# Loading the first half of the last V tile ahead of V tiles 29 and 30

## Chip, cores, metric

The kernel runs on one core of a Trainium2 chip. The metric is the device time of one execution in microseconds (us); lower is better. Before the change it was 1277.38 us (median of 3 runs, 1277.30 to 1277.45).

## The reference, cut

One token of a block that mixes a grouped-query attention over a long cache with a small gated MLP:

```python
# x: [1, 1, 448], bf16; 16 query heads, 8 KV heads, 65536 cached tokens, head size 256
def A(x, k_cache, v_cache, wq, wo):          # caches: [1, 8, 65536, 256] bf16, 268 MB each
    q = (x @ wq).reshape(...)                # 16 heads
    p = softmax(q @ k.T / 16)                # over 65536 tokens
    return (p @ v).reshape(1, 1, 4096) @ wo
def B(x, W_gate, W_up, W_down):              # 448 -> 1792 -> 448, ReLU gate
    ...
g = sigmoid((x * gate_w).sum())
out = g * A(...) + (1 - g) * B(...)
```

What matters here: 537 MB of K and V have to be read once, and hardly anything is computed per byte. Below, K31 or V29 is a tile of the K or V cache, numbered from 0 to 31 over all heads, and wo is the weight of the output projection.

## The kernel before

K and V come as 64 tiles of 8 MB (128 partitions x 64 KB): four K tiles and four V tiles for each of the eight KV heads. Three buffers of that size (`ring[0..2]`) take them in turn. All large loads are issued by the sync queue, in one order, each when the last reader of its buffer is done. The tail of that order is what the change touches (code abbreviated):

```python
TILE = 19.35                                  # us a tile is expected to take; only orders things
order = [("wq", 0, 8.7), ("k", 0, TILE), ("gu", 0, 7.7), ("wd", 0, 3.8)]
for n in range(1, NT):                        # NT = 32
    order.append(("k", n, TILE))
    if n >= NTH - 1:                          # NTH = 4; V lags K by three tiles
        order.append(("v", n - (NTH - 1), TILE))
NW = H - 3
order += [("wo", 0, 7.3), ("v", NT - 3, TILE), ("v", NT - 2, TILE)]
PIECES = [(0, 64), (64, 96), (96, 112), (112, 120), (120, 128)]   # V tile 31 comes in pieces
for i, (lo, hi) in enumerate(PIECES):
    order.append(("vp", i, TILE * (hi - lo) / U))
# ... cut: four more wo pieces, the last heads ...

# which buffer: a tile gets the next in turn, and waits for that buffer's last reader
LASTS = (0, 1, 2, 0, 1, 0)
if kind in ("k", "v") or (kind, i) in (("wo", 0), ("vp", 0)):
    sl = ...
    slot[kind, i], freed[kind, i] = sl, held.get(sl, [])
    held[sl] = [(kind, i)]
# so: K31 in 0, V28 in 1, wo in 2, V29 in 0 (after K31), V30 in 1 (after V28), V31's pieces in 0 (after V29)
wo_sb = ring[slot["wo", 0]][:, 0:J * 2 * D]   # wo fills 14336 of a row's 32768 elements: the rest is free

# ... cut ...
dep = dma("sp", t, "r%d" % sl, lambda e: e.dma_start(ring[sl][:], v_src(n)), free(("v", n)))
# ... cut: pieces of V31 ...
dep = dma("sp", t, "vp%d" % i, lambda e: e.dma_start(
    ring[sl][:, lo * 256:hi * 256], v_src(n)[:, lo * 256:hi * 256]), free(("vp", 0)))
# wo: five loads; rows of 1792 bytes, 128 partitions x 2 or 1 or, the first, 10 of them
l_["wo", i] = dma("sp", t, "wo%d" % i, lambda e: e.dma_start(wo_sb[:, lo:hi, :, :], ...), free(("wo", 0)))
```

TensorE multiplies a V tile as soon as it has landed and the head's probabilities are ready; the very last work is the projection of the last head with the last wo piece, a copy, and the store of 896 bytes.

## Time and profile before

| | value | where it stands |
|---|---|---|
| time | 1277.38 us | median of the runs |
| span in the profile | 1276.1 us | page |
| share of the span in which the 16 DMA engines move the sync queue's packets | 99.7% | page, part 3 |
| read from memory | 549.03 MB, 430 GB/s | page, part 3 |
| TensorE, VectorE busy | 33%, 50% | page, part 1 |

From the page of the kernel before: the span, TensorE's busy time, the 40 slices of the DMA engines' busy share (tenths) and of their rate, the main queue, and the chain that ended last.

```profile
span 1276.1 us, 10216 instructions
...
PE 427.3 (33%) x4568; PEld 167.5 (13%) x4568; DVE 633.2 (50%) x421; ACT 63.3 (5%) x124; POOL 4.6 (0%) x21
...
DMA  9999999999999999999999999999999999999998
GB/s 401 448 427 428 436 431 440 433 429 431 436 438 436 428 429 438 436 436 429 429 438 431 438 433 429 433 436 434 436 431 429 436 433 436 433 431 436 405 446 354
...
q1 hardware_dynamic: 12930, 549.03, 99.7%
...
HBM read 549.03 MB, written 0.00 MB: 430 GB/s over the span
## 4 chain that ended last, share of the span: by engine, by line
DMA 2%; PE 1%; SPq 0%; issue 0%; DVE 0%
DMA ring<-in_A_wo_dram 2%; PE O L409 1%; SPq L554 0%; PE A_ps L389 0%; SPq L563 0%; DVE P_sb L582 0%
```

Every slice of the DMA row is a 9, which is the highest digit, until the last.

The sync queue's timeline in the tail (start, how long the issue took, line; an issue waits for a free buffer ahead of its start). L550 are whole V tiles, L554 the pieces of V31, L563 wo:

```profile
...
start us, us, engine line op out<-in xcount [idle before <-releaser]
1172.85 0.33 SPq L550 DMA_DIRECT2D ring<-in_A_v_cache_dram  x1
1173.22 0.44 SPq L563 DMA_DIRECT2D ring<-in_A_wo_dram  x1
1208.27 13.83 SPq L550 DMA_DIRECT2D ring<-in_A_v_cache_dram  x2
1238.01 2.34 SPq L554 DMA_DIRECT2D ring<-in_A_v_cache_dram  x5
1240.39 21.26 SPq L563 DMA_DIRECT2D ring<-in_A_wo_dram  x4
```

At 1208.27 us V29 is issued, when K31's buffer comes free (the row merges two issues; the second, V30, starts at 1221.77). Of the end of the chain of waits (start, length, what):

```profile
...
1241.26 31.47 DMA ring<-in_A_wo_dram
...
1272.77 1.68 PE A_ps L389 x10
...
1274.48 0.38 DVE P_sb L582
```

The last wo piece lands at 1273.86 us (table below), and only 2.2 us follow it; what ends the kernel is when the last pieces land.

The page's shares are means over 16 engines. The trace says more: a transfer runs on all 16 DMA engines, and each adds one to the transfer's semaphore when its part has landed. The Trainium skill says so too ("DMA: Bandwidth & Descriptors", "Why a DMA increments its semaphore by 16 and not by 1": the engines "finish independently"). From these sixteen increments I take the first, the mean and the last for each transfer, in us. This table is worked out from the trace, it is no view of the profile:

```
before            first     mean      last     last minus first
V28             1203.18   1204.19   1206.13    2.94
wo, 10 heads    1209.19   1210.13   1211.92    2.73
V29             1229.56   1230.01   1231.28    1.72
V30             1249.02   1249.54   1250.72    1.70
V31, half       1258.71   1259.25   1260.42    1.71
last wo piece   1272.25   1272.77   1273.86    1.60
```

The sixteen engines are not level: one is 2.9 us behind the first. And the spread falls from 2.73 to 1.72 us at V29, because the engines that lead had run dry before V29's packets came.

### The profile page before, as it was taken

Reading aid. Unit: us, or ns where it says so; the run is one execution under the profiler, and the core shown is the slowest. Engines: PE = TensorE matmul, PEld = TensorE weight load, DVE = VectorE, ACT = ScalarE, POOL = GpSimd, SP = SyncE. Lnnn points to the kernel's source line nnn. Section 1 sums busy time; section 2 is a strip of 40 time slices with the busy share of each in tenths; the row PEclk is TensorE's granted clock in tenths of the full one; section 3 lists DMA queues with packets and bytes.
Section 4 is the critical chain, followed back from the end, with each engine's and each line's share of the span. In section 5 each row is a group of like instructions: output and inputs, shape, how many; then the busy total and the mean of one; then the engine's idle time right before and its main releaser. Section 6 shows DMA issues by size and latency. Waiting matters only on the chain. (4 is left out here: it accounts for less than half of the span.)

```text
span 1276.1 us, 10216 instructions
## 1 busy us (share of the span) xinstructions
PE 427.3 (33%) x4568; PEld 167.5 (13%) x4568; DVE 633.2 (50%) x421; ACT 63.3 (5%) x124; POOL 4.6 (0%) x21
## 2 busy tenths in 40 slices
PE   3633322334123532224331343321333324233254
PEld 1501110111001210002110111110111101011021
DVE  2597633465533655434555444555434655335600
ACT  0001000010000100001000010000100001000000
POOL 1000000000000000000000000000000000000000
PEclk9656666656666575667656666656666656666576
DMA  9999999999999999999999999999999999999998
GB/s 401 448 427 428 436 431 440 433 429 431 436 438 436 428 429 438 436 436 429 429 438 431 438 433 429 433 436 434 436 431 429 436 433 436 433 431 436 405 446 354
DMA packets 12948, 549.22 MB, mean 430 GB/s; under 512 B 1283, under 2 KB 3590, under 8 KB 3974
## 3 DMA queue, kind: packets, MB, share of 16 engines
q1 hardware_dynamic: 12930, 549.03, 99.7%
q8 instruction: 8, 0.13, 0.0%
q14 instruction: 6, 0.05, 0.0%
q10 hardware_dynamic: 4, 0.00, 0.0%
HBM read 549.03 MB, written 0.00 MB: 430 GB/s over the span
## 5 line engine op out<-in xcount | busy, mean ns | idle before, releaser
L367 DVE STREAM_TRANSPOSE ring<-ring 128x2048 uint32<-128x2048 uint32 x256 | 565.4, 2275 | 398.9 <-DMA ring<-in_A_k_cache_dram 398.9
L378 PE MATMUL ST<-ring,xc 128*16 128x512 bf16 x2048 | 222.8, 608 | 745.5 <-PEq L86 745.5
L378 PEld LDWEIGHTS ST<-ring,xc 128*16 128x16 bf16 x2048 | 68.0, 120 | 886.1 <-issue 884.8
L409 PE MATMUL O<-ring,ptp 128*4 128x512 bf16 x2048 | 152.3, 461 | 32.9 <-DMA ring<-in_A_v_cache_dram 18.8
L494 ACT ACTIVATE P_sb<-ST,nmb 128x512 bf16<-128x512 f32 x32 | 45.2, 1412 | 1103.5 <-DVE nmb L492 1103.5
L492 DVE TENSOR_REDUCE nmb<-ST 128x1 f32<-128x512 f32 x32 | 22.1, 689 | 116.8 <-PE ST L378 116.8
L409 PEld LDWEIGHTS O<-ring,ptp 128*4 128x4 bf16 x2048 | 56.9, 100 | 128.1 <-issue 71.8
L419 DVE CAST o_sb<-O 128x512 bf16<-128x512 f32 x8 | 5.5, 692 | 76.8 <-PE O L409 76.8
L513 DVE TENSOR_TENSOR P_sb<-P_sb,hs 128x1024 bf16<-128x1024 bf16 x16 | 18.9, 1222 | 9.4 <-ACT hs L507 9.4
L518 PE MATMUL PT<-identb,P_sb 128*128 128x128 bf16 x128 | 16.2, 307 | 16.8 <-PEq L86 15.8
L459 PE MATMUL M_ps<-xT,ring 128*128 128x1 bf16 x84 | 9.5, 205 | 17.5 <-DMA ring<-in_B_W_up_dram 17.5
L518 PEld LDWEIGHTS PT<-identb,P_sb 128*128 128x128 bf16 x128 | 12.4, 138 | 19.2 <-issue 19.2
L527 ACT COPY ptp<-PT 128x256 bf16<-128x256 bf16 x32 | 10.3, 375 | 23.9 <-PE PT L518 23.9
L341 PE MATMUL QN<-ring,P_sb 128*128 128x512 bf16 x32 | 8.9, 446 | 3.8 <-DMA ring<-in_A_wq_dram 3.8
L459 PEld LDWEIGHTS M_ps<-xT,ring 128*128 128x128 bf16 x84 | 7.2, 152 | 18.1 <-issue 17.7
L494 ACT ACTIVATION_READ_ACCUMULATOR P_sb<-ST,nmb 128x1 f32 x32 | 8.4, 263 | 0.0
L462 PE MATMUL M_ps<-xT,ring 128*64 128x1 bf16 x56 | 7.8, 276 | 0.0
L442 DVE STREAM_TRANSPOSE scr<-P_sb 128x256 uint32<-128x256 uint32 x1 | 0.4, 445 | 13.1 <-ACT P_sb L441 13.1
L503 PE MATMUL M_ps<-identf,hs 128*2 128x128 f32 x8 | 2.5, 308 | 11.1 <-PEq L86 11.1
L539 DVE RECIPROCAL hs<-M_ps 128x2 f32<-128x2 f32 x8 | 1.4, 171 | 8.3 <-PE M_ps L538 8.3
L462 PEld LDWEIGHTS M_ps<-xT,ring 128*64 128x64 bf16 x56 | 5.4, 191 | 0.4
L389 PE MATMUL A_ps<-ring,attnT 128*1 128x224 bf16 x64 | 4.7, 304 | 0.6 <-DMA ring<-in_A_wo_dram 0.6
(74 smaller groups left out, 66.2 us busy)
## 6 DMA issues: line engine op xcount, KB each, us to landing
ring<-in_A_v_cache_dram SPq DMA_DIRECT2D x1, 4096.0 KB, 22.4
ring<-in_A_wq_dram SPq DMA_DIRECT2D x1, 3072.0 KB, 10.4
ring<-in_A_wo_dram SPq DMA_DIRECT2D x1, 2240.0 KB, 38.7
ring<-in_A_v_cache_dram SPq DMA_DIRECT2D x1, 2048.0 KB, 26.9
ring<-in_B_W_down_dram SPq DMA_DIRECT2D x1, 1568.0 KB, 22.0
ring<-in_B_W_gate_dram SPq DMA_DIRECT2D x1, 1344.0 KB, 32.3
ring<-in_B_W_up_dram SPq DMA_DIRECT2D x1, 1344.0 KB, 35.1
ring<-in_A_v_cache_dram SPq DMA_DIRECT2D x1, 1024.0 KB, 28.9
```

The lines of the kernel that those rows point to most:

```text
L341: ins = e.matmul(QN_ps, xw3[:, k_, 31 - h:159 - h], rhs, start=(h == 0 and kt == 0), stop=(h == H - 1 and kt == R3))
L367: return lambda e: e.transpose(v, v)
L378: ins = e.matmul(bank[32 * w:32 * w + 16, :], xc[:, x0:x0 + 16], ktv[sl][:, u0:u0 + 16, c, :, r_], start=(b == 0 and c == 0 and r_ == 0), ...
L409: ins = e.matmul(OP[32 * g:32 * g + 4, :], ptp[:, col:col + 13:4], ring[sl][:, k * 512:(k + 1) * 512], start=(a == 0 and k < 4), stop=(a = ...
L419: o1 = op("dv", tn, lambda e: e.tensor_copy(o_sb[:], OP[:]), [pv[n], last.get(("otr", h - 1))])
L459: e.matmul(GU_ps[:, c:c + 1], wf3[which][:, kt * F + ft:(kt + 1) * F:FT], xT[:, kt:kt + 1], start=(kt == 0), stop=False, skip_group_check= ...
L462: ins = e.matmul(GU_ps[64 * half:64 * half + 64, c:c + 1], wfh[which][:, ft:F // 2:FT], xT[:, R3 + half:R3 + half + 1], start=False, stop= ...
L492: smax[n] = op("dv", tk + 22, lambda e, n=n, NM=NM, t_=t_: e.tensor_reduce(NM[:, t_:t_ + 1], ST[n % 2][:], AX.X, ALU.max, negate=True), [q ...
L494: aexp[n] = op("ac", tk + 23, lambda e, n=n, t_=t_, NM=NM, RS=RS: e.activation(P_sb[:, t_:2048:4], ST[n % 2][:], ACTF.Exp, bias=NM[:, t_:t ...
L513: rsc = op("dv", tt, lambda e, X=X, pb=pb: e.tensor_tensor(pb, pb, X[:, 12:16].unsqueeze(1).to_broadcast([128, 256, 4]), ALU.mult), [h7, a ...
L518: ins = e.transpose(PT[rd][:, s * 128:(s + 1) * 128], P_sb[:, (rd * 8 + s) * 128:(rd * 8 + s + 1) * 128], identb[:, :])
L527: ins = e.copy(dst, src)
```

## The change

The intent: give V29 more lead, that is, more time from its issue until the engines run out of earlier work. Its issue at 1208.27 us comes when the work ahead of it lasts only until 1209.2 (first engine) to 1211.9 us (last). The wo buffer has room for half a V tile behind wo, and that room is free at 1173 us. So the first half of V31 is loaded there, ahead of V29 and V30, and 9.7 us of work lie between. The bytes stay the same.

```diff
-        order += [("wo", 0, 7.3), ("v", NT - 3, TILE), ("v", NT - 2, TILE)]
-        PIECES = [(0, 64), (64, 96), (96, 112), (112, 120), (120, 128)]
+        order += [("wo", 0, 7.3), ("vp", 0, TILE / 2), ("v", NT - 3, TILE), ("v", NT - 2, TILE)]
+        PIECES = [(0, U // 2), (64, 96), (96, 112), (112, 120), (120, 128)]
         for i, (lo, hi) in enumerate(PIECES):
-            order.append(("vp", i, TILE * (hi - lo) / U))
+            order += [("vp", i, TILE * (hi - lo) / U)] if i else []
@@
-            if kind in ("k", "v") or (kind, i) in (("wo", 0), ("vp", 0)):
+            if kind in ("k", "v") or (kind, i) in (("wo", 0), ("vp", 1)):
@@ the matmuls of V take an offset into the buffer
-                                   ring[sl][:, k * 512:(k + 1) * 512],
+                                   ring[sl][:, base + k * 512:base + (k + 1) * 512],
@@
-                    sl = slot["vp", 0]
-                    dep = dma("sp", t, "vp%d" % i, lambda e, ...: e.dma_start(
-                        ring[sl][:, lo * 256:hi * 256], v_src(n)[:, lo * 256:hi * 256]), free(("vp", 0)))
+                    sl, base = (slot["wo", 0], J * 2 * D) if i == 0 else (slot["vp", 1], 0)
+                    assert base + hi * 256 <= U * DH
+                    dep = dma("sp", t, "vp%d" % i, lambda e, ...: e.dma_start(
+                        ring[sl][:, base + lo * 256:base + hi * 256], v_src(n)[:, lo * 256:hi * 256]),
+                        free(("vp", 1) if i else ("wo", 0)))
```

(The rest places the half tile's matmuls between those of V29 and V30.)

More of the change, by code (lines that the diff above doesn't have):

```diff
@@ L400, in free, with make_pv @@
             return out_
-        def make_pv(n, lo, hi, sl, tv, dep):
+        def make_pv(n, lo, hi, sl, tv, dep, base=0):
             h, a = divmod(n, NTH)
@@ L552, in bass_gated_mix__gqa_block_cached__glu_gated_reglu__decode_kernel @@
                     n, (lo, hi) = NT - 1, PIECES[i]
-                    sl = slot["vp", 0]
-                    dep = dma("sp", t, "vp%d" % i, lambda e, sl=sl, n=n, lo=lo, hi=hi: e.dma_start(
-                        ring[sl][:, lo * 256:hi * 256], v_src(n)[:, lo * 256:hi * 256]), free(("vp", 0)))
-                args = (n, lo, hi, sl, tL[kind, i], dep)
+                    sl, base = (slot["wo", 0], J * 2 * D) if i == 0 else (slot["vp", 1], 0)
+                    assert base + hi * 256 <= U * DH
+                    dep = dma("sp", t, "vp%d" % i, lambda e, sl=sl, n=n, lo=lo, hi=hi, base=base: e.dma_start(
+                        ring[sl][:, base + lo * 256:base + hi * 256], v_src(n)[:, lo * 256:hi * 256]), free(("vp", 1) if i else ("wo", 0)))
+                args = (n, lo, hi, sl, tL[kind, i], dep) if kind == "v" else \
+                    (n, lo, hi, sl, tL[kind, i] if i else tL["v", NT - 3] + 9, dep, base)
                 if ("tev", n // NTH) in last:
```

## The prediction

> **What bounds the kernel now.** The DMA engines. The slices of the page show all 16 busy at nine tenths or more until the last slice; the queue table gives queue 1 99.7% of their span, 549 MB at 430 GB/s. TensorE is busy 33%. The rate is near the 435 GB/s ceiling that the Trainium skill states ("DMA: Bandwidth & Descriptors", Specifications); this trace agrees. The chain of waits that ended last is almost one DMA wait: 31.5 us for the last wo piece.
>
> **Where the change could gain.** Only where an engine runs dry. Before, V tile 29 is issued at 1208.27 us, when k tile 31 frees its buffer (timeline), while the work queued ahead of it (V28, ten heads of wo) lasts until 1211.9. The trace has sixteen landing increments per transfer, one per DMA engine: the first wo piece lands from 1209.2 to 1211.92 us, V29 from 1229.6 to 1231.28; the spread falls from 2.7 to 1.7. So the early engines did wait about 1 us for the V29 issue. But the engine that lands last did not: from 1211.92 to 1231.28 are 19.36 us, eight 64 KB packets of 2.42 us each (packet records), with nothing between. It stays gapless to the end (V30 1250.72, half tile 1260.42, last wo piece 1273.86). The kernel ends with the slowest DMA engine, and that one never starves.
>
> **What the change does.** No byte, matmul or instruction is added; only the sync queue's order changes. It moves 4 MB, 9.7 us of all engines, ahead of V29. V29 then has about 12.7 us of lead instead of 3.6; it lands about 9.7 us later (1241.0), V30 at about 1260.4; the smaller pieces and the wo pieces land as before (1265.3 to 1273.9). V30's 64 matmuls (5.4 to 6.8 us) now run at 1260.4 to about 1267, so TensorE meets the first quarter piece 0.5 to 2 us late, but catches up by the last piece at 1270.4.
>
> On the critical path: nothing removed, nothing added. The 1 us saved on the early engines makes them finish earlier and wait for the late ones.
>
> **Side effects.** The half tile's issue probably blocks the sync queue from about 1173.7 until roughly 1204 to 1208 us: before, at 1241.7, an issue behind two small-row wo issues stood for 15.7 us. Nothing else is due there before 1208, so it is harmless. An instruction fetch (16 KB, 0.9 us at 1241.6) takes one engine's time; were it to fall on the slowest engine in the new timing, it would cost about 1 us.
>
> **Predicted time:** 1277.4 us, 1276.5 to 1278.2 for 8 in 10. Faster by over 2%: 0.005; within 2%: 0.99; slower by over 2%: 0.005.
>
> **What would show it.** V29's last landing near 1241 and V30's near 1260.4; landing spread after wo staying near 2.7 to 2.9 us instead of falling to 1.7; last wo landing within 0.5 us of 1273.9; the half tile's matmuls before V30's; the chain of waits still ending in the last wo piece.
>
> **What would make it wrong.** A fetch hitting another engine (about 1 us either way); the blocked issue delaying V29 beyond 1221 us (a gap on all engines); the late TensorE work or a lower granted clock outlasting the wo landing (up to 1 us); packet rates that depend on how many engines are active, so that the idle I dismiss turns into time (up to 1.2 us gained).

## The result

| | before | after |
|---|---|---|
| median of 6 runs | 1277.41 us | 1277.51 us |
| lowest to highest | 1277.26 to 1278.05 | 1277.43 to 1278.29 |
| span in the profile | 1276.1 us | 1276.2 us |

The ratio is 1.0001, 95% interval 0.9988 to 1.0014. (Ratios are the mean time of one kernel's runs over that of the other's of the same rounds, so not quite the ratio of the medians that are quoted.) The time is the same.

From the page after:

```profile
span 1276.2 us, 10216 instructions
...
DMA  9999999999999999999999999999999999999998
GB/s 402 447 427 428 435 440 433 431 429 435 429 442 433 428 431 435 438 433 431 429 435 435 433 433 429 435 435 432 438 429 435 429 438 438 429 431 433 416 443 346
...
q1 hardware_dynamic: 12930, 549.03, 99.7%
...
## 4 chain that ended last, share of the span: by engine, by line
DMA 2%; PE 1%; SPq 0%; DVE 0%; issue 0%
DMA ring<-in_A_wo_dram 2%; PE O L409 0%; PE A_ps L389 0%; SPq L555 0%; DVE P_sb L584 0%; PE M_ps L424 0%
```

The sync queue's timeline in the same stretch (L555 are now the pieces of V31, L565 wo):

```profile
...
1173.40 0.44 SPq L565 DMA_DIRECT2D ring<-in_A_wo_dram  x1
1173.88 29.89 SPq L555 DMA_DIRECT2D ring<-in_A_v_cache_dram  x1
1208.25 14.03 SPq L550 DMA_DIRECT2D ring<-in_A_v_cache_dram  x2
1246.59 1.75 SPq L555 DMA_DIRECT2D ring<-in_A_v_cache_dram  x4
1248.38 13.40 SPq L565 DMA_DIRECT2D ring<-in_A_wo_dram  x4
```

The half tile's issue at 1173.88 us stands for 29.89 us, as announced, and does no harm: V29 is issued at 1208.25 us, the same moment as before. The end of the chain of waits:

```profile
...
1248.38 23.39 DMA ring<-in_A_wo_dram
...
1271.82 0.91 PE A_ps L389 x8
...
1272.92 1.63 PE A_ps L389 x16
...
1274.58 0.38 DVE P_sb L584
```

The view follows another of the last wo pieces back, but the end is made of the same parts. TensorE's timeline in between shows the half tile's matmuls (at 1248.40) ahead of V30's (from 1260.63), and no late work at the end; the last line is the weight load for the last wo piece, which waits for its landing:

```profile
...
1248.40 1.96 PE L409 MATMUL O<-ring,ptp 128*4 128x512 bf16 x30
1260.63 0.10 PEld L409 LDWEIGHTS O<-ring,ptp 128*4 128x4 bf16 x8 [10.79 <-DMA ring<-in_A_v_cache_dram]
...
1268.07 0.60 PE L409 MATMUL O<-ring,ptp 128*4 128x512 bf16 x8 [0.81 <-DMA ring<-in_A_v_cache_dram]
...
1273.97 0.12 PEld L389 LDWEIGHTS A_ps<-ring,attnT 128*1 128x1 bf16 x4 [0.26 <-DMA ring<-in_A_wo_dram]
```

The landings per engine, again worked out from the trace:

```
after             first     mean      last     last minus first   last, against before
V28             1202.96   1204.13   1206.10    3.14               -0.03
wo, 10 heads    1208.96   1210.14   1212.11    3.14               +0.19
V31, half       1218.68   1219.85   1221.84    3.16
V29             1238.03   1239.21   1241.19    3.16
V30             1257.43   1258.74   1260.59    3.16
last wo piece   1270.89   1272.19   1273.93    3.03               +0.07
```

This is where the expected gain went. The spread stays at 3.1 us: no engine runs dry any more. The first engine finishes its part of the last wo piece 1.36 us earlier than before (1270.89 against 1272.25), and the mean of the sixteen 0.58 us earlier (1272.19 against 1272.77). The last engine finishes at 1273.93 instead of 1273.86. The change gave time to the engines that lead, and these then wait for the last one.

### The profile page after: what moved, and what is told of

Read it like the earlier page. It is cut to its first block, busy times and chain, and to the rows that moved or that the text cites. A ratio compares the mean times of both kernels' runs of the same rounds, so it can differ in the third digit from the quotient of the medians.

```text
span 1276.2 us, 10216 instructions
## 1 busy us (share of the span) xinstructions
PE 426.3 (33%) x4568; PEld 167.4 (13%) x4568; DVE 633.2 (50%) x421; ACT 63.4 (5%) x124; POOL 4.3 (0%) x21
## 5 line engine op out<-in xcount | busy, mean ns | idle before, releaser
L409 PE MATMUL O<-ring,ptp 128*4 128x512 bf16 x2048 | 149.0, 453 | 36.5 <-PEq L86 23.8
L442 DVE STREAM_TRANSPOSE scr<-P_sb 128x256 uint32<-128x256 uint32 x1 | 0.4, 445 | 13.3 <-ACT P_sb L441 13.3
L505 PE MATMUL M_ps<-mx,nselT 2*128 2x1 f32 x16 | 3.6, 292 | 4.1 <-PEq L86 4.1
```

What stands on the lines that cost most here:

```text
L409: ins = e.matmul(OP[32 * g:32 * g + 4, :], ptp[:, col:col + 13:4], ring[sl][:, base + k * 512:base + (k + 1) * 512], start=(a == 0 and k < ...
```

## The experiments

My theory: the kernel ends with the slowest DMA engine, which has no gap before the change either; lead counts only once an issue comes so late that this engine runs dry. Rivals: (a) the tail has slack, so V29's issue time never mattered; (b) the engines share one rate, so what counts is the mean idle time or the bytes; (c) the change won about 1 us and lost it again, for instance to the standing issue.

In eleven runs I first moved V29's issue, then the standing issue, then the load of single engines. All gave a correct result. "Before" in a batch is 1277.5 us (medians 1277.48 to 1277.56).

### Making V29 late: e1 to e4

The edit, in the kernel before (e1, e2) and in the changed one (e3, e4), makes V29's load wait for one more operation; X is the last copy of the probabilities (e1, e3), the exponential of K31 (e2), or the matmuls of V28 (e4):

```diff
+    late = [X] if n == NT - 3 else []
-    dep = dma("sp", t, "r%d" % sl, lambda e: e.dma_start(ring[sl][:], v_src(n)), free(("v", n)))
+    dep = dma("sp", max([t] + [o.key + 0.05 for o in late]), "r%d" % sl,
+              lambda e: e.dma_start(ring[sl][:], v_src(n)), free(("v", n)) + late)
```

e1, before, 7.5 us late:

> The kernel before, with the V29 issue made to wait for the last copy of the transposed probabilities (about 1215.9 us instead of 1208.3). Theory (the end is the slowest DMA engine's gapless queue): data start about 2.2 us after the issue, at 1218.1, so the slowest engine, which ran out at 1211.92, now waits 6.2 us: time +6 us, to +7.8 us if the instruction fetch falls on an engine that has lost its lead; 1283.5 to 1285.2. Rival (slack in the tail absorbs a late V29, so that its lead never mattered): within 0.5 us of 1277.4.

e2, before, meant to be 2 us late:

> The kernel before, with the V29 issue waiting for the exponential of k tile 31 (about 1210.4 us, 2.1 us later than it was). Theory: data start at about 1212.6, 0.7 us after the slowest engine ran out: +0.7 us if nothing else happens, +2.1 us if the later instruction fetch falls on one of the engines that lost their lead (in the trace of before that engine ended V30 level with the slowest). Rival (tail slack): 0. Rival (all engines share one rate, so a gap costs its mean over the engines): about +2.1 us over before in any case.

e3, changed, 7.8 us late:

> The changed kernel with the same late V29 issue as e1 (about 1215.9 us). Theory: the half V tile keeps the engines busy from 1209 to 1218.7 (first engine) and 1221.8 (slowest), data of V29 start at about 1218.1, so nothing waits: 0.0 +- 0.3 us against the changed kernel, 1277.5, and 6 to 8 us faster than e1. Rival (tail slack): equal to e1.

e4, changed, 13 us late:

> The changed kernel with the V29 issue waiting for the matmuls of V28 (about 1222.0 us, just after the half tile has landed on the slowest engine at 1221.84). Theory: data start at about 1224.1, the slowest engine waits 2.3 us: +2.3 us, up to +3.9 us with the instruction fetch on an engine without lead: 1279.8 to 1281.4. Rival (tail slack): 1277.5.

Measured:

| | V29 issued at | time, median | range | against "before" of the batch (1277.52) |
|---|---|---|---|---|
| e1, before | 1215.82 | 1285.04 | 1284.99 to 1285.34 | +7.5 us |
| e2, before | 1211.91 | 1279.61 | 1279.30 to 1281.46 | +2.1 us |
| e3, changed | 1216.03 | 1277.36 | 1277.34 to 1277.59 | -0.2 us |
| e4, changed | 1220.86 | 1281.12 | 1280.34 to 1281.41 | +3.6 us |

The sync queue's timeline of e1, from the first wo heads to V29 (and, merged, V30):

```profile
...
1174.30 0.44 SPq L564 DMA_DIRECT2D ring<-in_A_wo_dram  x1
1215.82 5.53 SPq L551 DMA_DIRECT2D ring<-in_A_v_cache_dram  x2
```

and of e3, where V29 comes as late and costs nothing:

```profile
...
1173.50 0.43 SPq L566 DMA_DIRECT2D ring<-in_A_wo_dram  x1
1173.97 29.89 SPq L556 DMA_DIRECT2D ring<-in_A_v_cache_dram  x1
1216.03 6.36 SPq L551 DMA_DIRECT2D ring<-in_A_v_cache_dram  x2
```

The last landings show what was paid. In e1 wo lands at 1212.09 and V29 at 1237.62: 25.53 us, where a tile takes 19.36, so 6.2 us too many. The sum is the expected one, but not all of it is idle time. By the packet records (a packet is one row of a load: 64 KB for a tile, 1792 bytes for wo) the slowest engine's last wo packet ends at 1211.63, and V29's first packets start from 1216.79 to 1217.62, the earliest 1.0 us after the issue and not 2.2; then the first packet of each engine takes 2.60 to 3.42 us instead of 2.42. So 5.2 to 6.0 us were waiting, and the rest slow first packets. V30 then lands at 1258.31, 20.69 us later, another 1.3 us. After V29 the engines stand within 0.54 us of one another; after V30 one alone is 1.1 us behind the rest. In that stretch the records have a 16 KB instruction fetch of 0.94 us (1249.19); the skill names such blocks ("Runtime: NRT & Kernel Launch", "Instruction fetch mechanics"). It fits: followed packet by packet, the engine with this fetch is the one that lands last, and its next 64 KB packet takes 2.91 us instead of 2.42, so the fetch costs it 1.4 us in all. No run took the fetch away. In e3 one of the engines that lead by 2.5 to 3 us loses about 1.5 us in the same stretch, and the end doesn't feel it.

So rival (a) falls: lead has a price as soon as it is gone, 7.5 us in e1. The same lateness is free in the changed kernel. e2 doesn't separate my theory from rival (b), for both allowed +2.1 us; its profiled run was also its slowest (1281.46), with the slowest engine 2.7 us behind the next already at K31. K31 landed 1.4 us late there, and V29's issue came 1.5 us later than the 1210.4 us reckoned, so I draw nothing more from it. In e4 the issue came 1.1 us earlier than I had reckoned; from the half tile's last landing to V29's are 20.72 us and from there to V30's 20.89, 1.4 and 1.5 us too many. Of the 1.4 us, 0.5 to 1.3 us were waiting (the last packet of the half tile ends at 1221.33, V29's start from 1221.81 to 1222.66), the rest slow first packets, of up to 3.29 us; in V30 it is again the engine with the fetch that lands last. The sum, 2.9 us, is near the 2.8 us by which that profiled run (1280.34, the fastest of e4) was slower than before.

### The standing issue: e5

```diff
-order += [("wo", 0, 7.3), ("vp", 0, TILE / 2), ("v", NT - 3, TILE), ...
+order += [("vp", 0, TILE / 2), ("wo", 0, 7.3), ("v", NT - 3, TILE), ...
```

> The changed kernel with the half V tile issued ahead of the first wo heads instead of behind them. In the changed kernel's trace the half tile's issue stands for 29.9 us behind the small rows of wo. Theory (no DMA engine ever waits for that issue): the issue takes 0.3 to 0.5 us, nothing else changes, time 1277.5 +- 0.3 us, V29 lands near 1241.2. Rival (the change won about 1 us and the standing issue gave it back): 1276.5.

Measured: 1277.51 us (1277.43 to 1277.56). The timeline of e5:

```profile
...
1173.90 0.43 SPq L555 DMA_DIRECT2D ring<-in_A_v_cache_dram  x1
1174.38 0.43 SPq L565 DMA_DIRECT2D ring<-in_A_wo_dram  x1
1208.23 14.35 SPq L550 DMA_DIRECT2D ring<-in_A_v_cache_dram  x2
```

The issue of 29.9 us is gone (0.43 us for each of the two), and the time is that of the changed kernel. The standing has moved to V29's own issue, behind wo now: in the trace it takes 5.3 us, and the last row merges it with V30's. That also costs nothing. Rival (c) falls for the standing issue.

### Extra work for some engines: e6 to e8, badly sized

If the slowest engine alone sets the end, useless loads on other engines must be free. A load of k partitions should run on k engines: the skill ("DMA: Bandwidth & Descriptors", the same section) says k is the largest number up to 16 that divides the slowest dimension of both sides, and that these are the lowest-numbered engines. The traces agree on the number: in e7 to e10 a load of k partitions has k landings. The loads go to the 4 KB that are still free behind the half tile:

```diff
+    for x, k in enumerate(KS if i == 0 else ()):
+        extra.append(dma("sp", t - 0.5 + 0.01 * x, "x%d" % x, lambda e: e.dma_start(
+            ring[slot["wo", 0]][16 * x:16 * x + k, 30720:32768], v_src(NT - 1)[16 * x:16 * x + k, 30720:32768]), ...))
```

with KS = (16, 16, 16, 16) in e6 and (8, 8, 8, 8) in e7; e8 has k = 1 to 15, packed without gaps.

> The changed kernel plus four useless loads of 16 partitions x 4 KB before the first wo heads (256 KB, 4 packets of 0.16 us on each of the 16 DMA engines, as one 4 KB packet takes in the trace). Theory and rival alike: every engine is 0.64 us longer, time +0.64 us, about 1278.1. It is the measure for the next run.

> The same with 8 partitions instead of 16 (128 KB; the landing increments should show only eight engines 0.64 us later). Theory (the slowest engine alone sets the end): either 0.0 us (the slowest engine is not among the eight: they catch up on their lead of 0.7 us or more) or the full +0.64 us (it is among them), not between. Rival (the engines share one rate, and bytes are what is paid): half of the run with 16, +0.32 us.

> The changed kernel plus 15 useless loads of 1, 2, ... 15 partitions x 4 KB before the first wo heads, to find out which engine is the slowest. If a load of k partitions runs on k engines, always the same first ones, the first engine gets 15 extra packets of 0.16 us (2.4 us), the last none (480 KB in all). Theory: the time rises by the extra of the slowest engine, 0.16 us times its number of packets, or by less than 1.7 us for engines whose lead is smaller than their extra; which of them moved stands in the landing increments. Rival (bytes are paid by all alike): 480 KB at 430 GB/s, +1.1 us, with all engines moved alike.

Measured: e6 1280.25 us (+2.7 against 1277.56), e7 1279.00 us (+1.4), e8 1281.24 us (+3.7). All three expectations of size missed. The packet records say why: the 64 extra packets of e6 took 0.241 us in the mean and up to 0.369, not 0.160, and 64 KB packets of V28 beside them up to 4.13 us instead of 2.42. The extra loads wrote neighbouring partitions. The skill ("SBUF — State Buffer", "Door 1: The DMA port swizzle") says that DMA bandwidth depends on how many of the 16 ports the partitions reach, and by its mapping 16 neighbours reach four. No trace here shows the ports; that e9 and e10 below, spread by this mapping, ran undisturbed fits it. So every engine was disturbed, and e7, at half of e6, decides nothing between my theory and rival (b).

e8 was still good for something. The last landings of the loads of 1, 2, 3 and 4 engines were 1204.34, 1204.61, 1204.86 and then 1208.04 us, and every wider load ends with such a late landing too. If the engines are taken in the skill's order, the fourth is the late one.

### Extra work again, without the disturbance: e9 and e10

Eight loads of 3 (e9) or 4 (e10) partitions x 4 KB, each partition four apart from the next, so that by the skill's mapping each engine writes its own port:

```diff
+    for x in range(8) if i == 0 else ():
+        p = slice(x % 4 + 32 * (x // 4), x % 4 + 32 * (x // 4) + 4 * K - 3, 4)      # K = 3 or 4
+        extra.append(dma("sp", ..., lambda e: e.dma_start(ring[slot["wo", 0]][p, 30720:32768], v_src(NT - 1)[p, 30720:32768]), ...))
```

> The changed kernel plus eight useless loads of 3 partitions x 4 KB before the first wo heads (96 KB), each partition four apart from the next. The useless loads of e6 to e8 wrote neighbouring partitions and their packets took up to twice their usual 0.16 us and slowed the packets beside them; these should not. In e8 the landing of the load on 4 engines was the first to come late (1208.0 us against 1204.9 for the one on 3), so the slowest engine is the fourth. Theory: three leading engines get 8 packets of 0.16 us (1.3 us) more, less than their lead of 2.5 us or more: time 0.0 us (+-0.3) against the changed kernel's 1277.5. Rival (shared rate, bytes are paid): +0.2 us; if small loads disturb every engine as in e6 to e8: +1 us.

> The same with 4 partitions instead of 3 (128 KB), so that the fourth engine gets its 8 packets too. Theory: the slowest engine is 1.3 us longer: +1.3 us, about 1278.8, of which e9 shows nothing. Rival (bytes are paid): +0.3 us, and no step between e9 and this run.

Measured: e9 1277.41 us (1277.37 to 1277.81), e10 1278.62 us (1278.59 to 1278.97), before 1277.48 us. The extra packets now took 0.160 us each, as they should. The landings, in us (from the trace; the lead of the second-last is how far it is ahead of the last):

```
                  wo last    lead of      last wo piece:
                             second-last  mean      last
changed kernel    1212.11    0.74         1272.19   1273.93
e9, 3 engines     1212.09    0.89         1272.37   1273.89
e10, 4 engines    1213.40    2.03         1272.52   1275.13
```

Three engines with 1.3 us of additional work each: the mean of the landings moves, the end does not. The fourth engine with the same: +1.2 us. Rival (b) says +0.2 and +0.3 us, with no step between; the step is there. In both runs the kernel's end is the end of one engine's queue, and this engine is the fourth.

### A version meant to beat both: e11

If one engine is late, take work from it. Of the second small piece of V31, 16 of the 128 rows go in loads of 3 partitions and 1 that run on the first engines only; the other 112 rows make 7 packets per engine instead of 8:

```diff
+    rows = [slice(0, 128)] if i != 2 else \
+        [slice(16, 128)] + [slice(r, r + 9, 4) for r in range(4)] + [slice(12, 15), slice(15, 16)]
+    for x, p in enumerate(rows):
+        dep = dma("sp", t + 0.01 * x, "vp%d" % i, lambda e: e.dma_start(ring[sl][p, ...], v_src(n)[p, ...]), ...)
```

> A version meant to beat both: the changed kernel, but 16 of the 128 rows of the second small piece (8 KB each) go in loads of 3 partitions and 1, which run on the first engines only; each of the 16 engines has 7 packets of 0.31 us for the rest instead of 8, the first three 5 or 6 more. Theory: the slowest engine is one packet shorter, the first three use 1.3 to 1.6 us of a lead of 2.1 us or more: -0.3 us, 1277.2; the last wo piece lands near 1273.6 instead of 1273.9. Rival (bytes are paid): 0.0. A gain this small may drown in the spread of the runs (0.2 us); then the landing decides.

Measured: 1281.17 us (1280.62 to 1281.49), 3.7 us slower than before. The 8 KB packets took 0.613 us in the mean, where they take 0.314 in the changed kernel (e11 ran on another chip than e1 to e10; its "before" was run again there), and 16 KB packets beside them up to 1.81 us instead of 0.62. Most of those packets belong to the load of 112 rows; my reading is that its sevens of rows no longer fall on one port per engine, as the eights of a 128-row load do. That is argued from the skill's mapping and from the contrast of e6 with e9, not shown by itself. Whether a rebalancing that keeps each engine on its own port would bring its 0.3 us stays open; I know none that can take work from the fourth engine alone.

## Why the prediction was right

- **The step that carried it**: the slowest engine had no gap to fill (19.36 us from wo to V29, eight packets of 2.42 us). Right: V29's issue now comes 13.6 us before that engine is out of work instead of 3.6 (the prediction said 12.7; 3.6 plus the half tile's 9.7 would have been 13.3), and the engine's last landing moved by +0.07 us. e9 and e10 show that in the changed kernel one engine alone sets the end; e1 and e3 show that the half tile does what it was meant for, once there is a gap to fill.
- **What held only just**: the prediction says that the engine which lands last never starves, to the end. By the packet records that is so up to V29. From V30 on, before the change, two engines are level: the gapless one lands V30 at 1250.65 us, and another at 1250.72. That other one had run dry before V29, had a slow first packet (3.15 us) and then carried the 16 KB fetch at 1241.59 us. So gap, slow packet and fetch together had used up this engine's lead, and at the end there were at most 0.09 us to win (1273.86 against 1273.77). That the fetch fell on an engine with just enough lead is luck; the prediction had listed it as a risk of about 1 us.
- **What happens to the time saved on the others**: right, with a number now: 0.58 us in the mean of the engines, 1.36 us on the first, nothing on the last.
- **Landings**: V29 1241.0 expected, 1241.19 measured; V30 1260.4 and 1260.59; last wo piece 1273.9 and 1273.93. The spread was to stay at 2.7 to 2.9 us and stayed at 3.1 (it was 3.1 from V28 on in this run).
- **The standing issue**: expected from 1173.7 until 1204 to 1208 us; it stood from 1173.88 to 1203.77. Harmless, as e5 shows by taking it away.
- **TensorE's late work**: V30 and the next piece were done at 1267.3 us, and TensorE waited for the following one at 1268.07. No effect.
- **What I had listed as a risk and did come, in small**: packet rates that depend on how many engines work. The ten wo heads took the slowest engine 6.01 us in the changed kernel and 5.79 before, when others had run dry. The other traces agree: 5.71 to 5.80 us where nothing was queued behind wo (before, e1, e2), 6.01 to 6.02 us where the half tile was (changed kernel, e3, e4, e11). So the engines are not quite independent, and to this extent rival (b) stands. It is 0.2 us, and against the change; the four last wo pieces gave 0.16 us back (3.30 instead of 3.46 us from the last V piece to the last landing).

## What to carry to other kernels

When a kernel is bound by DMA, look at the landings engine by engine before spending work on lead: a gap on the engines that are ahead cost nothing here, as long as it didn't use up their lead, and the mean busy share can't tell it from one on the engine that is behind. Lead is an insurance; the changed kernel forgives an issue 7.8 us late (e3) that costs the other 7.5 us (e1), and where issue times vary that may be reason enough to keep it. Small loads on neighbouring partitions (e6, +2.7 us for 256 KB that should take 0.6) and a load cut at 112 rows (e11, +3.7 us with no byte added) cost far more than their bytes; that the ports are the reason is argued, not shown.

## What the Trainium skill lacked or had wrong

- "DMA: Bandwidth & Descriptors", "Latency and other measured facts", says that engines 7 and 15 are usually slower, with a guess at the cause that concerns loads issued from GpSimd. What it lacks is that the 16 engines move apart in steps and stay so: from 0.45 us at the first K tile to 2.9 us in the tail of the kernel before, with the last one alone by 0.9 us. Here the late one is the fourth from the lowest (e9, e10), and it is behind rather than slow: its tiles take 19.36 us like those of the others. In one step, before the change, an engine carries an 8 KB fetch of 0.33 us at 868 us, its next 64 KB packet takes 3.08 us instead of 2.42, and from then on it is the last by 0.9 us (20.25 us from one last landing to the next instead of 19.36).
- "DMA: Bandwidth & Descriptors", Specifications: it gives about 358 GB/s as the limit of memory for one core, without the condition that the same page states under "Bandwidth": that this is each core's part when both cores of a pair stream. This kernel reads 430 GB/s over its whole span on one core; the 435 GB/s given there for the fabric is the figure that agrees.
- The same page on how a load is split over k engines: the runs agree (a load of 4 partitions reaches the fourth engine, one of 3 does not: +1.2 against 0.0 us). It doesn't warn that packets can take twice their time when a load of 128 rows is cut into other numbers of rows (0.61 instead of 0.31 us in e11); "SBUF — State Buffer" has the port map from which one can guess it.
- No page that I read gives the depth of the sync queue's descriptor rings. Here an issue stood for 29.9 us behind 80 small rows per engine (the changed kernel) and for 15.7 us in the tail before; that it waits there for room in a ring is my reading, and no run tested it.
